# A DeltaNet and MLP kernel: the second MLP product as seven products of blocks, with its sums on GpSimd, other DMA queues, and the inverse's rows behind marked adds

## The chip, the cores and the metric

The kernel runs on one core of a Trainium2 chip. The metric is device time in microseconds, the median of three runs. All data is fp32.

## The reference

What is computed, cut to the lines that matter (B, H, S, D = 4, 8, 768, 48; the model width is H * D = 384 and the hidden width 1536):

```python
k_n = k / (np.linalg.norm(k, axis=-1, keepdims=True) + 1e-06)
state = 0                                   # (B, H, D, D)
for t in range(S):
    y[:, :, t] = einsum('bhd,bhde->bhe', q[:, :, t], state)
    v_old = einsum('bhde,bhd->bhe', state, k_n[:, :, t])
    state = state + beta[t] * einsum('bhd,bhe->bhde', k_n[:, :, t], v[:, :, t] - v_old)
x = y as (B, S, H * D)
xn = (x - mean(x)) / sqrt(var(x) + 1e-06) * g_ln
out = x + maximum(xn @ w_ch1, 0) @ w_ch2
```

## The kernel before, in words

The sequence is cut into 12 chunks of 64 tokens. Two chunks make a slab. For each chunk the recurrence over its 64 tokens is turned into matrix products with the inverse of a triangular matrix, for all 32 pairs of batch and head. The chunk's tokens of all four batches (256 rows) then go through layer norm and the MLP.

The stages, by name:

- **Loads.** `load_turned` fetches keys and queries of a chunk in small blocks (tile `tb`, line 168), the keys on GpSimd's queue and the queries on SP's. `load_kv` fetches keys and values (lines 184, 175) on SP. `turned` (L348) transposes `tb` into `kqt` on VectorE.
- **Gram matrices.** `gram` (L368) multiplies keys by keys into `p_g`; ScalarE copies them to `gsb` (L376, L383). `product` (L393, L395) does the same for keys and queries and masks the result into `pt`.
- **Inverse.** `blocks` and `inverse` (L477 to L560) invert the 32x32 triangles of a slab on VectorE, one row at a time: a product into `tmp` (L555), a subtraction from `xb` (L560), each with two SBUF inputs, 31 times, two rows to a step. `scatter` (L483, L468, L472) turns the result into `xt`. `join` (p_e L580, p_z L626) then combines two 32x32 triangles into the 64x64 one on TensorE.
- **Recurrence.** `recur`: p_k and p_y from the state (L652), `v_raw` minus p_k on VectorE (L657), p_u (L663), p_s (L675) and its add to the state `s_all` on VectorE (L678), p_y (L683), layer norm (L694 to L701), the transposes p_n (L709) into `xnt`.
- **MLP.** `ffn`: for each of 12 blocks of the hidden width, p_h = W1 block by `xnt`, 3 products of 128x256 (L724), and ScalarE's ReLU into `h_f` (L730). Then h W2: for each half of 128 rows, 12 products of 128x384 that add up in one PSUM tile p_o (L746); VectorE adds x (L735) and SP's queue stores `o` (L737). Chunk 0 does both halves together. The PSUM tiles p_h and p_o share a pool with two buffers.

The norms of the keys (L411 to L420) and the scaling of v by them (L428, on GpSimd) are prepared a chunk or more ahead.

What sets the order: `Plan` is a list of due times, in units of which one chunk has T = 45. Every stage is a generator with a number of steps spread over a stretch of the plan; the steps are traced in the order of their due times, and the scheduler of the framework orders each engine's instructions by this priority and by when it believes them ready. An engine runs its queue strictly in the order so fixed. `tc.issue_after(ins)` puts what is traced in a block behind `ins` on `ins`'s engine; `behind_each(tc, last, gen)` does so for every step of a generator, with the instructions that `last` holds at that moment. Before the change only `join` is so treated, behind the MLP's latest product.

The lines of the plan that the change and the prediction speak of:

```python
times = (t - 70, t - 58, t - 18, t - 13) if m > 2 else (t - 56, t - 46, t - 18, t - 13)
plan.spread(in_turn(*(prep_g(c) for c in chunks)), SLAB * 2, times[0], times[1])
plan.spread(blocks(m), N_BLOCKS, times[1], times[2])
joining = join(chunks)
plan.spread(joining if m == 1 else behind_each(tc, mlp, joining), 3, times[3], t - 2)
```

Here t is the start of the slab's first chunk in the plan and m is the slab.

## Time and profile before

| what | value |
|---|---|
| median of 3 runs | 614.44 us (612.59 to 615.7) |
| span of the profiled execution | 613.5 us |
| passes of p_h (L724), 128x256 | 864, busy 206.9 us |
| passes of p_o (L746), 128x384 | 576, busy 201.2 us |
| VectorE's rows (L555 and L560) | 42.3 and 51.1 us busy |
| GpSimd: v by its norm (L428), 128x768 | 10 of 1.476 us |
| GpSimd: key loads (L168) | 64, busy 42.6 us |
| DMA | 34.51 MB, 56 GB/s over the span |

How to read it: PE is TensorE's products and PEld its weight loads, which run beside them; DVE is VectorE, ACT ScalarE, POOL GpSimd, SP the queue of SyncE. A product of fp32 shows as two records. The mean length of a matmul's record is a latency, and records overlap, so what one costs is read from a stretch in which nothing else runs. A group's line gives busy time and mean length, then the engine's idle time just before it and what ended that idle time.

### The profile page before, as it was taken

The numbers are of one execution on the slowest core, as the hardware profiler recorded it, in microseconds if no ns is written. First come the engines' busy times: TensorE is split into PE (matmuls) and PEld (weight loads), VectorE is DVE, ScalarE is ACT, GpSimd is POOL, SyncE is SP. The second block draws the span as 40 slices with busy tenths as digits, with TensorE's granted clock in tenths as the row PEclk, the third lists the DMA queues.
The fourth block names the chain that finished last, engine by engine and source line by source line (L and its number), as shares of the span: only waits on it lengthen the run. The fifth ranks groups of instructions, "written<-read, shape, count | busy, mean of one in ns | idle before, by whom it ended". The sixth has DMA issues, their size and how long they took to land.

```text
span 613.5 us, 20905 instructions
## 1 busy us (share of the span) xinstructions
PE 540.2 (88%) x9512; PEld 403.8 (66%) x9512; DVE 322.7 (53%) x681; ACT 170.4 (28%) x351; POOL 80.7 (13%) x128
## 2 busy tenths in 40 slices
PE   2046886988999959999999999999999999999997
PEld 2035765556767846866767867768768678677673
DVE  5846868992246992239964059952179720201000
ACT  1223242402333214241224242242322142122120
POOL 5000116321041202300303200011000010000000
PEclk9999878998999979999999999999999999999999
DMA  4817889326044601411600500200200000000101
GB/s 54 199 50 164 172 179 243 56 52 95 3 97 62 103 8 24 74 34 28 104 16 17 101 16 15 53 16 15 53 14 15 1 22 9 14 15 1 27 1 26
DMA packets 126919, 34.51 MB, mean 56 GB/s; under 512 B 121184, under 2 KB 124272, under 8 KB 126832
## 3 DMA queue, kind: packets, MB, share of 16 engines
q1 hardware_dynamic: 110256, 19.14, 18.7%
q0 software_dynamic: 3504, 10.25, 6.0%
q10 hardware_dynamic: 13072, 3.80, 2.7%
q8 instruction: 74, 1.21, 0.8%
q14 instruction: 13, 0.11, 0.1%
HBM read 28.44 MB, written 4.72 MB: 54 GB/s over the span
## 4 chain that ended last, share of the span: by engine, by line
PE 55%; DVE 28%; issue 6%; DMA 3%; ACT 3%; SPq 3%; POOL 1%; ACTq 0%; DVEq 0%; POOLq 0%
PE p_o L746 19%; PE p_h L724 19%; DVE tmp L555 8%; DVE xb L560 8%; SPq L168 2%; PE p_g L368 2%; PE p_y L683 2%; PE p_e L580 2%; DVE kqt L348 2%; PE p_z L626 2%; PE p_g L393 1%; PE p_u L663 1%; DVE own L483 1%; PE p_n L709 1%; PE p_s L675 1%
## 5 line engine op out<-in xcount | busy, mean ns | idle before, releaser
L724 PE MATMUL p_h<-xnt,w_sb 128*128 128x256 f32 x864 | 206.9, 393 | 5.9 <-DVE o L735 5.2
L746 PE MATMUL p_o<-w_sb,h_f 128*128 128x384 f32 x576 | 201.2, 498 | 0.0
L724 PEld LDWEIGHTS p_h<-xnt,w_sb 128*128 128x128 f32 x864 | 164.4, 195 | 34.0 <-DVE o L735 4.0
L746 PEld LDWEIGHTS p_o<-w_sb,h_f 128*128 128x128 f32 x576 | 107.4, 193 | 65.6 <-issue 3.0
L730 ACT ACTIVATE h_f<-p_h 128x256 f32<-128x256 f32 x144 | 55.3, 384 | 192.4 <-PE p_h L724 192.3
L168 POOL DMA_DIRECT2D tb<-in_k_dram x64 | 42.6, 673 | 110.8 <-DVE tmp L555 57.3
L560 DVE TENSOR_TENSOR xb<-xb,tmp 128x31 f32<-128x31 f32 (+20 forms) x154 | 51.1, 332 | 5.1
L735 DVE TENSOR_TENSOR o<-p_o,x_ln 128x384 f32<-128x384 f32 x24 | 13.2, 549 | 74.0 <-PE p_o L746 74.0
L555 DVE TENSOR_TENSOR tmp<-xb,gb 128x31 f32<-128x31 f32 (+15 forms) x124 | 42.3, 341 | 3.8
L694 DVE BATCH_NORM_STATS2 st<-x_ln 128x6 f32<-128x384 f32 x24 | 12.3, 547 | 49.4 <-ACT x_ln L688 49.4
L678 DVE TENSOR_TENSOR s_all<-s_all,p_s 128x768 f32<-128x768 f32 x11 | 10.4, 942 | 47.2 <-PE p_s L675 47.1
L348 DVE STREAM_TRANSPOSE kqt<-tb 128x1024 f32<-128x1024 f32 x24 | 29.3, 1232 | 4.1 <-DMA tb<-in_k_dram 3.8
L368 PE MATMUL p_g<-kqt 48*64 48x64 f32 (+2 forms) x1024 | 16.8, 239 | 12.3 <-DVE kqt L348 8.2
L368 PEld LDWEIGHTS p_g<-kqt 48*32 48x32 f32 (+1 forms) x1024 | 14.8, 133 | 17.8 <-DVE kqt L348 8.3
L610 PE MATMUL p_e<-x_n,gsb 32*32 32x16 f32 x512 | 6.0, 187 | 21.6 <-DVE x_n L605 17.3
L420 POOL TENSOR_SCALAR knrm<-knrm 128x16 f32<-128x16 f32 x12 | 3.1, 257 | 163.1 <-ACT knrm L419 163.1
L417 DVE TENSOR_REDUCE ksum<-ksq 128x8 f32<-128x384 f32 x22 | 12.1, 550 | 21.2 <-ACT ksq L411 10.9
L580 PE MATMUL p_e<-x_n,gsb 32*32 32x32 f32 x768 | 16.1, 200 | 7.7 <-DVE mv L695 5.8
L580 PEld LDWEIGHTS p_e<-x_n,gsb 32*32 32x32 f32 x768 | 14.7, 113 | 11.0 <-DVE x_n L574 6.0
L393 PEld LDWEIGHTS p_g<-kqt 48*64 48x64 f32 x768 | 14.0, 142 | 11.9 <-DVE s_all L678 6.4
L657 DVE TENSOR_TENSOR v_raw<-v_raw,p_k 128x768 f32<-128x768 f32 x11 | 10.5, 952 | 20.8 <-PE p_k L652 20.8
L393 PE MATMUL p_g<-kqt 48*64 48x64 f32 x768 | 16.5, 231 | 5.1 <-DVE s_all L678 3.8
(99 smaller groups left out, 509.9 us busy)
## 6 DMA issues: line engine op xcount, KB each, us to landing
words<-in_moe_w_ch_dram POOLq DMA_DIRECT2D x9, 768.0 KB, 5.9
out_dram<-o SPq DMA_DIRECT2D x48, 96.0 KB, 2.2
k<-in_k_dram SPq DMA_DIRECT2D x44, 96.0 KB, 2.8
v_raw<-in_v_dram SPq DMA_DIRECT2D x22, 192.0 KB, 4.0
tb<-in_q_dram SPq DMA_DIRECT2D x44, 64.0 KB, 3.0
words<-in_moe_w_ch_dram ACTq DMA_DIRECT2D x3, 768.0 KB, 6.4
tb<-in_k_dram POOLq DMA_DIRECT2D x32, 64.0 KB, 3.4
tb<-in_q_dram SPq DMA_DIRECT2D x44, 32.0 KB, 2.6
```

The costliest lines, as they stand in the source:

```text
L168: engs[m % len(engs)].dma_start(out=dst[p0 : p0 + 32, :, u, 0:w], in_=src[:, hp::2, toks, 32 * m : 32 * m + w].rearrange("b j t d -> t (b ...
L348: nc.vector.transpose(made[c][0][:, :, n].rearrange("p i (u t) -> p i u t", t=32), tblocks[(2 * c + n) % NTB])
L368: nc.tensor.matmul(out_, kqt[rows, i, 0, r0 : r0 + (BK if fine else C)], kqt[rows, i, 0, r0:C])
L393: nc.tensor.matmul(p_g[half(e ^ hp), hp, j], kqt[rows, i, 0], kqt[rows, i, 1])
L555: nc.vector.tensor_tensor(out=t, in0=xb[:, :, 0:n, j : j + 1].to_broadcast([128, nb, n, w]), in1=gb[:, :, j : j + 1, j + 1 : L].to_broadca ...
L560: nc.vector.tensor_tensor(out=rest, in0=rest, in1=t, op=ALU.subtract)
L580: nc.tensor.matmul(p_e[r1, h], gsb[r0, h, BK:C], xn[r0, h])
L694: nc.vector.bn_stats(out=st[:, g], in_=y[:, g])
L724: nc.tensor.matmul(p_h, w1_sb[:, t, f * 128 : (f + 1) * 128], xnt[:, t], start=(t == 0), stop=(t == KC - 1),)
L730: nc.scalar.activation(h_f, p_h, ACTF.Relu)
L735: nc.vector.tensor_tensor(out=o, in0=p_o, in1=x[:, g], op=ALU.add)
L746: nc.tensor.matmul(p_o, hs[f][:, g * 128 : (g + 1) * 128], w2_sb[:, f], start=(f == 0), stop=(f == FT - 1),)
```

## The change

Five edits:

1. **h W2 as seven products.** For chunks 1 to 11, h (256 rows by 1536) and W2 (1536 by 384) are cut into 2 x 2 blocks, and the product is formed by Winograd's form of Strassen's scheme: seven products of blocks in place of eight. A block product is 6 products of 128x192 for one half of the rows, one half of the hidden width and one half of the output columns. The sums of W2's blocks (t1 to t4) are made once by `sum_blocks`; the sums of h's blocks (s1 to s4) are made per chunk; both on GpSimd. VectorE adds the products to x in eight adds of 128x192. The PSUM tile p_a holds three products on top of one another; p_c and p_b are two halves of one tile, in one bank. h is kept in two tiles of six blocks each.
2. **Key loads** of `load_turned` go to SP's queue.
3. **Stores** of the result go to GpSimd's queue, except the last chunk's.
4. **The inverse's rows queue behind what TensorE waits for.** `soon()` marks a VectorE instruction (the subtraction of p_k, the add to `s_all`, the normalised rows, the adds of the MLP); each step of `blocks` is queued behind the one marked last.
5. **The plan:** T from 45 to 43, gram matrices and rows due up to 4 units later.

```diff
     def load_turned(c):
-        load_blocks(k, c, 0, (nc.gpsimd,))
+        load_blocks(k, c, 0, (nc.sync,))
         load_blocks(q, c, 1, (nc.sync,))
...
             nc.vector.tensor_tensor(out=v_j, in0=v_j, in1=p_k, op=ALU.subtract)
+            soon()
...
             nc.vector.tensor_tensor(out=s_all, in0=s_all, in1=p_s, op=ALU.add)
+            soon()
...
                 op0=ALU.subtract, op1=ALU.mult,
             )
+        soon()
...
-    N_FFN = FT + 2 * FT // 2
+    HF, HM = FT // 2, DM // 2
+    N_FFN = FT + 7 * 2
+    sums = []
+
+    def sum_blocks():
+
+        late = ctx.enter_context(tc.tile_pool(name="late", bufs=1))
+        b11, b12, b21, b22 = (w2_sb[:, i : i + HF, j : j + HM] for i in (0, HF) for j in (0, HM))
+        t2, t3, t4 = (late.tile([128, HF, HM], FP32, name=f"t{i}") for i in (2, 3, 4))
+        for t, x0, x1 in ((t3, b22, b12), (b12, b12, b11), (t2, b22, b12), (t4, b21, t2)):
+            nc.gpsimd.tensor_tensor(out=t, in0=x0, in1=x1, op=ALU.subtract)
+        sums.extend((late, b12, t2, t3, t4))
...
+    urgent = {}
+
+    def soon():
+        urgent["DVE"] = nc.cur_bb.bb.instructions[-1]
...
-            h_f = work.tile([128, TOK], FP32, name="h_f", bufs=FT)
-            nc.scalar.activation(h_f, p_h, ACTF.Relu)
-            hs.append(h_f)
+            nc.scalar.activation(h[f // HF][:, f % HF], p_h, ACTF.Relu)
...
+                (nc.gpsimd if c < NCH - 1 else nc.sync).dma_start(
+                    out=out[2 * e + g, c * C : (c + 1) * C, :], in_=os[g][e * C : (e + 1) * C]
                 )
...
+        def add(out_, in0, in1):
+            nc.vector.tensor_tensor(out=out_, in0=in0, in1=in1, op=ALU.add)
+            soon()
...
+        a11, a21, a12, a22 = (h[i][:, :, g * 128 : (g + 1) * 128] for i in range(2) for g in range(2))
+        late, t1, t2, t3, t4 = sums
+
+        s1, s2, s3, s4 = a21, a11, late.tile([128, HF, 128], FP32, name="s3"), a12
...
+        p_a, p_cb = ps_ffn([128, HM], "p_a"), ps_ffn([128, DM], "p_o")
+        p_c, p_b = p_cb[:, 0:HM], p_cb[:, HM:]
...
+        def mul(p, a, b, first):
+            for f in range(HF):
+                nc.tensor.matmul(
+                    p, a[:, f], b[:, f], start=(first and f == 0), stop=(f == HF - 1), skip_group_check=True,
+                )
+                mlp["PE"] = nc.cur_bb.bb.instructions[-1]
+                if f == HF // 2 - 1:
+                    yield
+
+        sum_of(s3, a11, a21, ALU.subtract)
+        sum_of(s1, a21, a22, ALU.add)
+        yield from mul(p_a, a11, w11, True)
+        add(o11, p_a, x11)
+        sum_of(s2, s1, a11, ALU.subtract)
+        yield
+        yield from mul(p_c, a12, w21, True)
+        add(o11, p_c, o11)
+        sum_of(s4, a12, s2, ALU.subtract)
+        yield
+        yield from mul(p_b, s1, t1, False)
+        add(o22, p_b, x22)
+        yield
+        yield from mul(p_a, s2, t2, False)
+        add(o12, p_a, x12)
+        yield
+        yield from mul(p_b, s4, w22, False)
+        add(o12, p_b, o12)
+        store(0)
+        yield
+        yield from mul(p_a, s3, t3, False)
+        add(o22, p_a, o22)
+        add(o21, p_a, x21)
+        yield
+        yield from mul(p_c, a22, t4, True)
+        add(o21, p_c, o21)
+        store(1)
+        yield
...
-    T = 45
+    T = 43
...
+    plan.once(42, sum_blocks)
...
-            times = (t - 70, t - 58, t - 18, t - 13) if m > 2 else (t - 56, t - 46, t - 18, t - 13)
+            times = (t - 70, t - 54, t - 14, t - 13) if m > 2 else (t - 56, t - 42, t - 14, t - 13)
...
-            plan.spread(blocks(m), N_BLOCKS, times[1], times[2])
+            plan.spread(behind_each(tc, urgent, blocks(m)), N_BLOCKS, times[1], times[2])
```

More of the change, by code (lines that the diff above doesn't have):

```diff
@@ L711, in recur @@
         yield
-    N_FFN = FT + 2 * FT // 2
+    HF, HM = FT // 2, DM // 2
[8 more added lines that the diff above has]
+        sums.extend((late, b12, t2, t3, t4))
     mlp = {}
+    urgent = {}
+    def soon():
+        urgent["DVE"] = nc.cur_bb.bb.instructions[-1]
     def ffn(c):
         xnt, x = xnts.pop(c), xs.pop(c)
-        hs = []
+        h = [work.tile([128, HF, TOK], FP32, name="h") for _ in range(2)]
         for f in range(FT):
@@ L728, in ffn, with store @@
             mlp["PE"] = nc.cur_bb.bb.instructions[-1]
-            h_f = work.tile([128, TOK], FP32, name="h_f", bufs=FT)
-            nc.scalar.activation(h_f, p_h, ACTF.Relu)
-            hs.append(h_f)
+            nc.scalar.activation(h[f // HF][:, f % HF], p_h, ACTF.Relu)
             yield
-        def store(g, p_o):
-            o = work.tile([128, DM], FP32, name="o", bufs=2)
-            nc.vector.tensor_tensor(out=o, in0=p_o, in1=x[:, g], op=ALU.add)
+        os = [work.tile([128, DM], FP32, name="o", bufs=2) for g in range(2)]
+        def store(g):
             for e in range(2):
-                nc.sync.dma_start(
-                    out=out[2 * e + g, c * C : (c + 1) * C, :], in_=o[e * C : (e + 1) * C]
-                )
-        for gs in ((0, 1),) if c == 0 else ((0,), (1,)):
-            p_os = [ps_ffn([128, DM], "p_o") for g in gs]
+                (nc.gpsimd if c < NCH - 1 else nc.sync).dma_start(
+                    out=out[2 * e + g, c * C : (c + 1) * C, :], in_=os[g][e * C : (e + 1) * C]
+                )
+        def add(out_, in0, in1):
+            nc.vector.tensor_tensor(out=out_, in0=in0, in1=in1, op=ALU.add)
+            soon()
+        if c == 0:
+            p_os = [ps_ffn([128, DM], "p_o") for g in range(2)]
             for f in range(FT):
-                for g, p_o in zip(gs, p_os):
+                for g in range(2):
                     nc.tensor.matmul(
-                        p_o, hs[f][:, g * 128 : (g + 1) * 128], w2_sb[:, f],
+                        p_os[g], h[f // HF][:, f % HF, g * 128 : (g + 1) * 128], w2_sb[:, f],
                         start=(f == 0), stop=(f == FT - 1),
@@ L752, in ffn, with sum_of @@
                     yield
-            for g, p_o in zip(gs, p_os):
-                store(g, p_o)
+            for g in range(2):
+                add(os[g], p_os[g], x[:, g])
+                store(g)
             yield
+            return
+        a11, a21, a12, a22 = (h[i][:, :, g * 128 : (g + 1) * 128] for i in range(2) for g in range(2))
+        late, t1, t2, t3, t4 = sums
+        s1, s2, s3, s4 = a21, a11, late.tile([128, HF, 128], FP32, name="s3"), a12
+        def sum_of(out_, in0, in1, op):
+            nc.gpsimd.tensor_tensor(out=out_, in0=in0, in1=in1, op=op)
+        p_a, p_cb = ps_ffn([128, HM], "p_a"), ps_ffn([128, DM], "p_o")
+        p_c, p_b = p_cb[:, 0:HM], p_cb[:, HM:]
+        x11, x12, x21, x22 = (x[:, g, n : n + HM] for g in range(2) for n in (0, HM))
+        o11, o12, o21, o22 = (os[g][:, n : n + HM] for g in range(2) for n in (0, HM))
+        w11, w21, w22 = w2_sb[:, 0:HF, 0:HM], w2_sb[:, HF:, 0:HM], w2_sb[:, HF:, HM:]
+        def mul(p, a, b, first):
[34 more added lines that the diff above has]
+        yield
     NW = len(pieces)
```

## The prediction

> **What bounds the kernel now.** I read the page's busy shares first, then the costliest groups, then the chain, then busy time by stretch, then TensorE's waits.
>
> From the page of the kernel before (parts 1 and 5):
>
> ```profile
> PE 540.2 (88%) x9512; PEld 403.8 (66%) x9512; DVE 322.7 (53%) x681; ACT 170.4 (28%) x351; POOL 80.7 (13%) x128
> ...
> L746 PE MATMUL p_o<-w_sb,h_f 128*128 128x384 f32 x576 | 201.2, 498 | 0.0
> ...
> L746 PEld LDWEIGHTS p_o<-w_sb,h_f 128*128 128x128 f32 x576 | 107.4, 193 | 65.6 <-issue 3.0
> ```
>
> TensorE leads. L746 is h W2: 576 records for 12 chunks x 12 blocks x 2 halves = 288 products, so each fp32 product is two passes. The 498 ns is a latency; passes overlap, so it is no price. The price comes from the chain in order of time, whose last two pieces run with nothing in between (start, length, what):
>
> ```profile
> 577.98 15.54 PE p_h L724 x72
> 593.52 15.49 PE p_o L746 x48
> ```
>
> 15.54/72 = 215.8 ns for a pass of 256 columns, 15.49/48 = 322.7 ns for 384. The difference is 0.835 ns a column and the rest 2.0 ns: TensorE is paced by columns and the weight loads are wholly hidden.
>
> Busy time by stretch, from one start of p_k to that two chunks later, then the last recurrences (bounds; length; PE, PEld, DVE, ACT, POOL busy; clock; DMA share; GB/s):
>
> ```profile
> 245.10:332.30 87.20, 84.88 (x1408) 63.00 (x1411) 50.26 (x110) 26.40 (x55) 14.77 (x21) 1.00 0.27 47
> 332.30:419.50 87.20, 84.73 (x1408) 63.04 (x1408) 50.30 (x110) 26.39 (x55) 9.61 (x13) 1.00 0.20 38
> ...
> 506.40:544.10 37.70, 37.70 (x451) 28.10 (x450) 5.29 (x11) 7.37 (x17) 0.00 (x0) 1.00 0.05 12
> ```
>
> A steady pair of chunks costs 87.2 us and TensorE idles 2.3 to 2.5 us of it. So the steady state is TensorE's, and the 28% of VectorE on the chain are mostly stretches where the two run side by side. TensorE's waits from 160 to 560 us (total, times, longest):
>
> ```profile
> PE p_e L580 <- DVE mv L695: 5.8, 1, 5.8
> PE p_g L393 <- DVE s_all L678: 3.8, 3, 1.4
> PE p_h L724 <- DVE o L735: 2.8, 3, 0.9
> ```
>
> All three are VectorE being late. The first is the second pair, where p_e waits for the transposed inverse. The other two are adds that TensorE waits for while the rows of the inverse stand in front of them.
>
> **What the Trainium skill says.** "TensorE: Matmul & The Clock Gate", LDWEIGHTS, prices a load at its columns over 1.2 GHz, 107 ns for 128. The trace has six transposes with one 128-column load each, about 109 ns apart (p_n: 0.82 us from first start to last end, 0.27 of it the latency of one), which agrees, though a transpose may load faster than a product. "SBUF — State Buffer", two separate sides, says that GpSimd and VectorE share a port pair as an exclusive lock, held for a whole instruction, against VectorE operations with two SBUF inputs. The trace agrees (timeline of the kernel before: start, length, engine, instruction):
>
> ```profile
> 128.49 0.29 DVE L560 TENSOR_TENSOR xb<-xb,tmp 128x126 f32<-128x126 f32 x1
> ...
> 128.97 1.48 POOL L428 TENSOR_TENSOR v_raw<-v_raw,knrm 128x768 f32<-128x768 f32 x1
> 129.13 1.46 DVE L560 TENSOR_TENSOR xb<-xb,tmp 128x120 f32<-128x120 f32 x1
> ```
>
> A row that takes 0.29 us takes 1.46 us and ends 0.14 us after GpSimd's product does. "PSUM — Partial Sum Buffer", bank collisions, wants PSUM guarded by bank, not by address. No wait of the kernel before shows two products in one bank.
>
> **The change part by part.**
>
> *h W2 as seven products (chunks 1 to 11).* Removed: 24 products of 384 columns, 48 passes x 322.7 = 15.49 us. Added: 7 x 6 = 42 products of 192 columns, 84 passes. By the line above a pass is 0.835 x 192 + 2.0 = 162.3 ns, so 13.63 us, if a load of 128 columns still hides. Lower bound of the load: 107 ns. Upper: loads of 64 columns in four tiles of the array (p_u, 64 in 1.08 us, so 16 per tile at 67.5 ns with their products) give at most 135 ns for 128. The worst reading is the whole latency, 190 ns. I take hidden: -1.86 us a chunk, -20.4 us for eleven. Chunk 0 is unchanged.
>
> *Adds on VectorE.* Two of 549 ns become eight of 192 columns. From 549 (384 columns) and 421 (own+p_z, 256) the slope is 1.0 ns, so 357 ns each: 2.86 - 1.10 = +1.76 us a chunk. VectorE would be at 53.8 of some 82 us a pair, so as a sum it is hidden.
>
> *Sums on GpSimd.* Four of 128x768, priced by L428 (1.475 us): 5.9 us a chunk on an engine with 10 to 15 us of work in 87. TensorE hides them: the first two products (3.9 us) need no sum; s3 needs only the first half of h; s1 is done about 2 us after h, s2 at about 3.5 us (needed at 5.9), s4 at about 5.5 us (needed at 7.8). The price falls on VectorE through the lock: up to 5.9 us of delay a chunk where rows run. The block sums of W2 (4 of 128x1152, some 2.2 us each by 1.92 ns an element) fall between the last reading of W2 by chunk 0 (131 us) and chunk 1's third product (after 167 us): hidden, with perhaps 1 to 3 us of lock before the p_e at 138.86.
>
> *A new wait in one bank.* p_c and p_b share a bank. If the wait is by bank, the third product waits for the add that reads the second: 0.2 us to drain, 0.36 us add, 0.05 us to restart, so 0.6 us a chunk, 6.6 us in all, if VectorE is free and nothing stands between. The plan puts other TensorE work into some of these gaps: I take half, +3.3. The other adds have one or two products (1.95 or 3.9 us) of room.
>
> *Rows behind the urgent adds.* The waits for s_all (3.8) and o (2.8) are taken away: -6.6. What queues behind each marked add is the next two rows (up to 1.8 us) and so the inverse, for which p_e waits. In the pair before 419 us, the second gram starts at 357.67 and ends at 358.75, x_n is done at 398.03 and p_e starts at 403.79: 39.3 us of chain and 5.8 us to spare. The plan has 48.3 units between that gram (t-59.5) and the join (t-11.2), 46.1 us as run. After: 44.8 units (gram at t-56), and with 84.8 - 3.7 = 81.1 us of TensorE for 86 units, 42.3 us. The chain gets +1.8 (adds), +2.4 (normalisation, which ran at 399 to 402, behind it) and 0 to 5.9 of lock: 43.5 to 49.4 us. It is late by 1.2 to 7.1 us a pair, unless TensorE has other products to run first, which near the end of a chunk it mostly has. I take 1.5 us for each of the three steady pairs and 1.5 more on the 5.8 of the second: +6.0.
>
> *Loads and stores.* Keys on SP: 8 more issues of about 0.6 us a chunk (SP's q loads: 13 in 7.95), some 13 us in 41; they run a chunk or more ahead: 0. Stores on GpSimd, 0.65 us an issue as its key loads have: SP no longer holds loads behind a store that waits for o (SP's q loads at 190.79 came right behind one at 188.85), and keys leave GpSimd in exchange: 0 for the sum, perhaps -1 in the second pair. T from 45 to 43 only moves the order.
>
> Sum: 614.4 - 20.4 + 3.3 - 6.6 + 6.0 = 596.7, so 597 us.
>
> **The rivals.**
>
> *All of it lands:* the adds come at once, the inverse stays ahead, the bank's wait lies beside other work: 614.4 - 20.4 - 6.6 = 587.4, about 588 us. For it: TensorE has 97% of the steady pairs. Against it: the chain's slack of 5.8 us is spent.
>
> *The inverse becomes the bound (slower):* the lock costs all of 5.9 us and TensorE has nothing else. Then 7.1 us for each of three pairs, as much more in the second, and the whole 6.6 of the bank: 614.4 - 20.4 - 6.6 + 28.4 + 6.6 = 622 us. For it: between 364 and 398 us VectorE is busy 31.87 of 34 us, and the lock is seen at 129. Against it: a row's order is chosen beside the products, and p_u comes well after p_e.
>
> *The weight loads show (slower):* a pass costs 190 ns, so 84 x 0.190 = 15.96 us, +0.47 a chunk, +5.2 in all; with +3.3, -6.6, +6.0 this is 622 us. Against it: the 109 and 67.5 ns above.
>
> **How the numbers follow.** Forecast 0.50, all lands 0.27, inverse bound 0.16, loads show 0.05, something in the order that I don't see 0.02. Within 0.5% is 611.4 to 617.5: between forecast and inverse bound, 0.09. Slower 0.14, faster 0.77. The range goes from 584 (all lands, and 3 us of the ramp through freer queues) to 614 (half-way to the inverse as bound); what is left out is the slower cases and a little below.
>
> **What would show it.** The last 84 passes in 13.6 us, in place of 48 in 15.5, show the price of a pass; 16 us would show the loads. Records of p_a and p_cb that wait for an add after the second product show the bank. The lines for s_all and o among TensorE's waits should be gone. A wait of p_e for x_n in every pair, and rows of 1.5 us beside GpSimd's sums, would show the inverse as the bound. The prediction fails if TensorE falls under 93% in the steady pairs, or if a sum comes late to its product.

## The result and the profile after

The change makes the kernel slower: 638.35 us median (636.51 to 641.14, 4 runs) against 613.52 us (611.08 to 615.7, 4 runs) for the kernel before on the same chip. The ratio is 1.041, with a 95% interval of 1.0351 to 1.0468. The forecast was 597 us, with a range of 584 to 614. Where single microseconds are compared below, they come from the profiled executions: a span of 613.5 us before and 639.4 us after. Each ratio compares a kernel's runs with those of the kernel before that were taken beside it (medians 615.4 to 616.5 us in the experiments), without the runs that are over 1.5% above the same kernel's quickest, so that where times spread, the median of all runs can lie above what the ratio says.

The page of the kernel after, parts 1 and 5. A group's line gives engine, operation, output <- inputs, shape and count, then busy time and mean ns, then the engine's idle time just before and what ended it:

```profile
PE 540.9 (85%) x9908; PEld 471.9 (74%) x9908; DVE 371.2 (58%) x747; ACT 169.9 (27%) x351; POOL 153.2 (24%) x156
...
L788 POOL TENSOR_TENSOR h<-h 128x768 f32<-128x768 f32 x33 | 60.1, 1821 | 129.0 <-ACT h L747 89.6
...
L560 DVE TENSOR_TENSOR xb<-xb,tmp 128x31 f32<-128x31 f32 (+20 forms) x154 | 61.8, 401 | 4.6
L555 DVE TENSOR_TENSOR tmp<-xb,gb 128x31 f32<-128x31 f32 (+15 forms) x124 | 54.0, 436 | 3.4
...
L788 POOL TENSOR_TENSOR s<-h 128x768 f32<-128x768 f32 x11 | 20.1, 1831 | 79.4 <-ACT h L747 79.4
```

Three things are to be seen. TensorE is as busy as before (540.9 us against 540.2), although 11 chunks have 1.86 us less of products each. GpSimd's sums take 1.82 us each, not 1.475. And the rows of the inverse, whose number and shapes have not changed, take 115.8 us (61.8 + 54.0) where they took 93.4 (51.1 + 42.3).

That the products themselves got cheaper is plain at the end of the chain in order of time (start, length, what):

```profile
631.12 1.95 PE p_a L798 x12
633.07 1.96 PE p_o L798 x12
```

12 passes of 128x192 in 1.95 us are 162.5 ns a pass; 162.3 was forecast. Busy time by stretch, with the columns of the forecast (bounds; length; PE, PEld, DVE, ACT, POOL busy; clock; DMA share; GB/s), for one steady pair of chunks and for the chunk after the last rows:

```profile
351.30:444.90 93.60, 85.29 (x1483) 75.87 (x1484) 58.53 (x122) 26.35 (x56) 23.16 (x21) 0.95 0.20 36
...
536.00:571.90 35.90, 35.90 (x487) 32.74 (x487) 6.89 (x17) 7.35 (x17) 9.37 (x8) 1.00 0.06 13
```

The second line is what the change was made for: 35.9 us in place of 37.7, TensorE never idle. There are no rows there. The first line is a pair with rows: 93.6 us in place of 87.2. TensorE idles 8.3 us of it (93.60 - 85.29) and its clock is 0.95. Its products should have kept TensorE busy for 84.7 - 3.7 = 81.0 us; it was busy for 85.3. So I put 4.3 us down to the lower clock and 5.8 us to more idling than the 2.5 of before: 87.2 - 3.7 + 4.3 + 5.8 = 93.6.

TensorE's waits from 160 to 572 us (total, times, longest), against 5.8, 3.8 and 2.8 us before:

```profile
PE p_g L393 <- DVE s_all L679: 12.2, 3, 5.4
PE p_e L580 <- DVE x_n L574: 11.6, 4, 4.1
PE p_o L798 <- DVE o L759: 6.2, 5, 3.0
```

All are VectorE being late, as before, but 30.0 us where those three lines had 12.4. The third is not the wait for `o` of before: that one was p_h's, and it fell from 2.8 to 0.9 us. This one is new. All five times it is the third block product (p_b) that waits until the add has read the second (p_c), the other half of the same tile; more on it below. Why VectorE is late can be read where the first of the pair's two long waits begins. VectorE's timeline of the kernel after (start, length, instruction):

```profile
408.96 0.38 DVE L560 TENSOR_TENSOR xb<-xb,tmp 128x207 f32<-128x207 f32 x1
409.37 1.84 DVE L555 TENSOR_TENSOR tmp<-xb,gb 128x192 f32<-128x192 f32 x1
411.25 1.84 DVE L560 TENSOR_TENSOR xb<-xb,tmp 128x192 f32<-128x192 f32 x1
413.02 0.94 DVE L679 TENSOR_TENSOR s_all<-s_all,p_s 128x768 f32<-128x768 f32 x1
```

GpSimd's timeline in the same stretch:

```profile
409.19 3.69 POOL L788 TENSOR_TENSOR h<-h 128x768 f32<-128x768 f32 x2 [8.57 <-ACT h L747]
```

TensorE's:

```profile
414.01 1.16 PE L393 MATMUL p_g<-kqt 48*64 48x64 f32 x64 [3.43 <-DVE s_all L679]
415.10 1.90 PE L798 MATMUL p_o<-w_sb,h 128*128 128x192 f32 x6
...
428.19 1.92 PE L580 MATMUL p_e<-x_n,gsb 32*32 32x32 f32 x64 [4.06 <-DVE x_n L574]
```

A row has two instructions of 0.38 us. Two sums start at 409.19, and for as long as they run the row's two instructions take 1.84 us each, 3.68 us in all beside GpSimd's 3.69. The add to `s_all` stands behind that row and comes 2.9 us later than it could, and TensorE has nothing else in front: it idles 3.43 us. The 64 products of p_g that come next still take 1.16 us, as at full clock; then six passes take 1.90 us where they take 1.14. After 4.06 us of idling, 64 products of p_e take 1.92 us where they take 1.20. That is the lower clock of the pair: the granted clock is 0.50 from 416 to 418 us and from 428 to 432 us. The Trainium skill has both halves of this: "SBUF — State Buffer", two separate sides (the lock, which the loser waits for to the end), and "TensorE: Matmul & The Clock Gate", What's actually happening, which puts the array at half its clock after an idle window of about 3.4 us. The two waits here are 3.43 and 4.06 us, and the trace agrees. But 3.4 us is no limit below which a wait is safe: in the kernel e1 below, 2.72 us of idling are followed by half clock as well (64 products of p_e in 1.92 us), while 2.45 us in e17 are not.

The same happens once more, early. VectorE in the ramp, at the first step of the second slab's inverse:

```profile
119.28 2.27 DVE L541 TENSOR_SCALAR nrm<-nrm 128x32 f32<-128x32 f32 x1 [0.32 <-ACT nrm L540]
...
122.19 2.49 DVE L545 TENSOR_TENSOR db<-db,beta_f 128x32 f32<-128x32 f32 x1
124.72 3.23 DVE L546 TENSOR_TENSOR xb<-xb,db 128x512 f32<-128x512 f32 x1
127.88 2.65 DVE L549 COPY xb<-db 128x32 f32<-128x32 f32 x1
```

These four stand beside the four sums of W2's blocks, which GpSimd runs from 118.70 to 130.47 us at 2.64 to 2.99 us each. Without neighbours the second, third and fourth take 0.19, 0.69 and 0.19 us (a kernel below shows it).

Where the 25.9 us lie, by stretch between starts of p_k, with two kernels from the experiments beside it (in after and e11 a part of chunk 4's p_k runs ahead; the start of the rest is taken):

| stretch (us) | before | after | after, no sums (e11) | half of the chunks (e9) |
|---|---|---|---|---|
| start to chunk 2 | 167.3 | 174.8 | 164.0 | 165.6 |
| chunk 2 to 4 | 77.7 | 82.6 | 77.3 | 73.4 |
| 4 to 6 | 87.2 | 93.8 | 86.1 | 84.8 |
| 6 to 8 | 87.2 | 93.6 | 87.8 | 84.9 |
| 8 to 10 | 86.9 | 91.2 | 85.6 | 84.2 |
| 10 to 11 (no rows) | 37.7 | 35.9 | 35.9 | 35.9 |
| 11 to the end | 69.4 | 67.5 | 65.7 | 67.5 |
| span | 613.5 | 639.4 | 602.4 | 596.3 |

The sums cost something even where no rows are left: in the last stretch the two normalised blocks of rows (L703) stand beside three sums and take 3.19 us, where e11 has 0.87.

### The profile page after: what moved, and what is told of

Same layout as the page of the kernel before. It is cut to its first block, busy times and chain, and to the rows that moved or that the text cites. A ratio compares the mean times of both kernels' runs of the same rounds, so it can differ in the third digit from the quotient of the medians.

```text
span 639.4 us, 21859 instructions
## 1 busy us (share of the span) xinstructions
PE 540.9 (85%) x9908; PEld 471.9 (74%) x9908; DVE 371.2 (58%) x747; ACT 169.9 (27%) x351; POOL 153.2 (24%) x156
## 4 chain that ended last, share of the span: by engine, by line
PE 50%; DVE 34%; issue 7%; ACT 3%; DMA 3%; POOL 1%; ACTq 0%; SPq 0%; DVEq 0%; POOLq 0%
PE p_h L742 20%; DVE tmp L555 9%; DVE xb L560 9%; PE p_o L798 8%; PE p_a L798 7%; PE p_e L580 2%; PE p_z L626 2%; PE p_g L368 2%; DVE o L759 2%; DMA tb<-in_k_dram 1%; PE p_y L685 1%; PE p_u L664 1%; DMA words<-in_moe_w_ch_dram 1%; DVE own L483 1%; DVE gb L477 1%
## 5 line engine op out<-in xcount | busy, mean ns | idle before, releaser
L747 ACT ACTIVATE h<-p_h 128x256 f32<-128x256 f32 x144 | 55.2, 383 | 181.5 <-PE p_h L742 181.4
L788 POOL TENSOR_TENSOR h<-h 128x768 f32<-128x768 f32 x33 | 60.1, 1821 | 129.0 <-ACT h L747 89.6
L798 PE MATMUL p_o<-w_sb,h 128*128 128x192 f32 x396 | 79.6, 349 | 6.6 <-DVE o L759 6.2
L798 PEld LDWEIGHTS p_o<-w_sb,h 128*128 128x128 f32 x396 | 69.4, 202 | 8.8 <-DVE o L759 6.1
L560 DVE TENSOR_TENSOR xb<-xb,tmp 128x31 f32<-128x31 f32 (+20 forms) x154 | 61.8, 401 | 4.6
L555 DVE TENSOR_TENSOR tmp<-xb,gb 128x31 f32<-128x31 f32 (+15 forms) x124 | 54.0, 436 | 3.4
L754 POOL DMA_DIRECT2D out_dram<-o x44 | 24.0, 549 | 85.5 <-DVE o L759 50.4
L759 DVE TENSOR_TENSOR o<-p_a,x_ln 128x192 f32<-128x192 f32 x33 | 11.6, 352 | 51.5 <-PE p_a L798 51.4
L788 POOL TENSOR_TENSOR s<-h 128x768 f32<-128x768 f32 x11 | 20.1, 1831 | 79.4 <-ACT h L747 79.4
L393 PE MATMUL p_g<-kqt 48*64 48x64 f32 x768 | 19.2, 253 | 19.5 <-DVE s_all L679 12.2
L798 PE MATMUL p_a<-t,h 128*128 128x192 f32 x132 | 28.7, 363 | 1.4 <-DVE o L759 1.0
L580 PEld LDWEIGHTS p_e<-x_n,gsb 32*32 32x32 f32 x768 | 16.1, 121 | 16.1 <-DVE x_n L574 12.1
L759 DVE TENSOR_TENSOR o<-p_o,o 128x192 f32<-128x192 f32 x33 | 11.4, 345 | 25.1 <-PE p_o L798 24.9
```

The source lines that it names most:

```text
L393: nc.tensor.matmul(p_g[half(e ^ hp), hp, j], kqt[rows, i, 0], kqt[rows, i, 1])
L555: nc.vector.tensor_tensor(out=t, in0=xb[:, :, 0:n, j : j + 1].to_broadcast([128, nb, n, w]), in1=gb[:, :, j : j + 1, j + 1 : L].to_broadca ...
L560: nc.vector.tensor_tensor(out=rest, in0=rest, in1=t, op=ALU.subtract)
L580: nc.tensor.matmul(p_e[r1, h], gsb[r0, h, BK:C], xn[r0, h])
L747: nc.scalar.activation(h[f // HF][:, f % HF], p_h, ACTF.Relu)
L754: (nc.gpsimd if c < NCH - 1 else nc.sync).dma_start(out=out[2 * e + g, c * C : (c + 1) * C, :], in_=os[g][e * C : (e + 1) * C])
```

## The experiments

The theory that I took from the two traces (the lock): GpSimd's sums stop VectorE whenever they meet it, and VectorE is what TensorE waits for. The rivals: the order of VectorE's work (eight adds, rows queued behind marks), the queues, the plan's due times, and, later, the seven products themselves.

### The sums taken away, and their waits kept

In e1 the four sums of h per chunk are left out; the products read the blocks of h as they are. The instructions on VectorE, ScalarE and SP and their order are the same as in the kernel after.

```diff
-        s1, s2, s3, s4 = a21, a11, late.tile([128, HF, 128], FP32, name="s3"), a12
+        s1, s2, s3, s4 = a21, a11, a11, a12
...
-            nc.gpsimd.tensor_tensor(out=out_, in0=in0, in1=in1, op=op)
+            pass
```

> The changed kernel without the four sums of h's blocks on GpSimd: s1 to s4 are left out, so TensorE multiplies the blocks of h as they are and the output is not the reference's. The queues of VectorE, ScalarE and SP are the same, instruction by instruction. Lock theory (GpSimd's sums hold the port that VectorE's rows need, the inverse comes late, TensorE idles and its clock falls): 598 to 610 us, VectorE's rows (L555 and L560) fall from 115.8 us to about 105 (the block sums of W2 still stretch slab 1's), steady pairs fall from 93.6 to 82 to 86 us. Order theory (the rows queued behind marked adds, and due 4 units later, are what makes the inverse late): 630 to 640 us.

Measured: 612.49 us, ratio 0.9931 (0.9904 to 0.9957). The page of e1:

```profile
L560 DVE TENSOR_TENSOR xb<-xb,tmp 128x31 f32<-128x31 f32 (+20 forms) x154 | 49.8, 324 | 4.6
L555 DVE TENSOR_TENSOR tmp<-xb,gb 128x31 f32<-128x31 f32 (+15 forms) x124 | 42.1, 340 | 3.4
```

The rows are back at 91.9 us. So nothing in the order, the queues or the plan made them longer. The time is 2.5 us above what the lock theory expected, and the pairs, at 87.3, 86.9 and 85.2 us, are above its 82 to 86: the sums are most of the loss, but something is left.

In e2 each sum is replaced by two memsets of the same tile (the sums are left out of the computation here too). The waits of the products for GpSimd stay, and GpSimd is busy 65.0 us with them (88 memsets of 0.74 us), but a memset reads nothing.

```diff
-            nc.gpsimd.tensor_tensor(out=out_, in0=in0, in1=in1, op=op)
+            nc.gpsimd.memset(out_, 0.0)
+            nc.gpsimd.memset(out_, 0.0)
```

> Each of the four sums of h's blocks is replaced by two memsets of the same tile (128x768) on GpSimd: the blocks hold zeros and the output is not the reference's, but TensorE still waits for GpSimd at the same four places, and GpSimd is busy for nearly as long. A memset reads nothing from SBUF. Lock theory: as without the sums, 598 to 612 us, no rows of 1.8 us. Wait theory (TensorE waits for GpSimd's sums as such): 625 us or more.

Measured: 617.02 us, ratio 0.9994 (0.9957 to 1.0032), 0.6% above e1, with the rows at 323 and 340 ns. This lies between the two expectations, 5 us above the one and 8 below the other. Being busy and being waited for is worth some 0.6% (two memsets take 1.48 us where a sum takes 1.82); the 4% from there to the kernel after come only with sums that read.

### The sums added to the kernel before

The counter-proof is e12: the kernel before, with four idle sums of 128x768 on GpSimd per chunk that nobody reads, in chunks 1 to 11. Its own products, adds, queues and plan stay.

```diff
+            for _ in range(4):
+                nc.gpsimd.tensor_tensor(
+                    out=scratch[0], in0=hs[FT - 1][:, None, :].to_broadcast([128, 3, TOK]),
+                    in1=w1_sb[:, 0, 0 : 3 * TOK].rearrange("p (a b) -> p a b", a=3), op=ALU.subtract,
+                )
```

> The kernel before with four sums of 128x768 added on GpSimd for each of chunks 1 to 11, of h's last block and a weight tile, whose results nobody reads; the products, adds, plan and queues of before. Lock theory: the rows beside the sums wait as in the kernel after, and the chain's spare 5.8 us are not enough for what the sums take (20 us over the run): 619 to 640 us. Rival (sums cost only what waits for them, as the products of after do): 613 to 616 us, since nobody waits for these.

Measured: 632.45 us, ratio 1.0268 (1.0221 to 1.0315). The sums alone make the kernel before slower, by about two thirds of what the whole change does. In the profiled run most of it lies in two stretches: chunk 2 to 4 (5.9 us) and the last pair with rows (7.9 us). The key loads, which stand behind the sums in GpSimd's queue here, are not the cause: VectorE waits 4.1 us for them over the run, 3.8 us in the kernel before. Its VectorE in the last pair, before TensorE's longest wait:

```profile
491.41 1.71 DVE L468 TENSOR_SCALAR xt<-own,is_u 128x512 f32<-128x512 f32 x1
493.05 2.02 DVE L472 COPY xt<-own 128x512 f32<-128x512 f32 x1
494.99 2.02 DVE L468 TENSOR_SCALAR xt<-own,is_u 128x512 f32<-128x512 f32 x1
496.93 2.02 DVE L472 COPY xt<-own 128x512 f32<-128x512 f32 x1
...
499.49 0.91 DVE L678 TENSOR_TENSOR s_all<-s_all,p_s 128x768 f32<-128x768 f32 x1
```

Its GpSimd:

```profile
491.04 7.62 POOL L739 TENSOR_TENSOR scratch<-h_f,w_sb 128x768 f32<-128x768 f32 x4 [33.99 <-ACT h_f L731]
```

Its TensorE:

```profile
500.46 1.99 PE L393 MATMUL p_g<-kqt 48*64 48x64 f32 x64 [7.40 <-DVE s_all L678]
```

Four instructions of 0.41 to 0.57 us in the kernel before (same lines, at 395 us) take 7.8 us beside four sums, one for one, and TensorE waits 7.4 us. L472 is a plain copy of one tile, so it isn't only instructions with two tiles as inputs that the sums stop.

### The sums of W2's blocks

In e10 one thing is moved: the four block sums are queued on GpSimd behind the start of the first inverse (after the memset of `es`) and no longer run at 118.7 us.

```diff
-    plan.once(42, sum_blocks)
+    def late_sums():
+        with behind(tc, joined):
+            sum_blocks()
+
+    plan.once(56, late_sums)
```

> The kernel after with one edit: the four sums of W2's blocks are queued on GpSimd behind the start of the first inverse, so that they do not run beside the second slab's first rows. Lock theory: the +7.5 us that the trace shows up to chunk 2's p_k become 0 to +2, and the steady pairs stay, so 629 to 634 us (ratio about 1.028). Rival (the ramp is late through the key loads on SP or through the first chunks' own adds): unchanged, 636 to 642 us.

Measured: 630.14 us, ratio 1.0243 (1.0201 to 1.0284). The ramp ends at 163.4 in place of 174.8 us. VectorE in e10, the instructions that were shown above:

```profile
117.03 0.19 DVE L545 TENSOR_TENSOR db<-db,beta_f 128x32 f32<-128x32 f32 x1
117.26 0.69 DVE L546 TENSOR_TENSOR xb<-xb,db 128x512 f32<-128x512 f32 x1
117.87 0.19 DVE L549 COPY xb<-db 128x32 f32<-128x32 f32 x1
```

So four sums at a bad moment, once in the run, cost 1.7%. The steady pairs stay at 93.9, 93.5 and 91.2 us, as they should.

In e11 neither the sums of h nor those of W2's blocks are left (the products read the blocks as they are).

```diff
-        t2, t3, t4 = (late.tile([128, HF, HM], FP32, name=f"t{i}") for i in (2, 3, 4))
-        for t, x0, x1 in ((t3, b22, b12), (b12, b12, b11), (t2, b22, b12), (t4, b21, t2)):
-            nc.gpsimd.tensor_tensor(out=t, in0=x0, in1=x1, op=ALU.subtract)
-        sums.extend((late, b12, t2, t3, t4))
+        sums.extend((late, b12, b22, b22, b21))
```

> The kernel after with neither the sums of h nor those of W2's blocks (its products read blocks of h and W2 as they are, so the output is not the reference's). Lock theory: against the kernel without the sums of h (ratio 0.993) the ramp's 5 to 7 us come as well: 603 to 607 us, ratio 0.982 to 0.988; what is then still missing to 594 (= 614.4 - 20.4) is the inverse's chain with its later start and p_e's waits of 2 to 3 us a pair. Rival (the block sums cost nothing): 0.990 to 0.996 again.

Measured: 607.09 us, ratio 0.9852 (0.9813 to 0.9891), as expected. From 1.041 to 0.985: all sums together cost 5.6% of the run, some 34 us. The rest, from 0.985 to the forecast's 0.97, is not the sums'.

### What the lock is not: queues, marks, the engine for the sums

e6 takes key loads and stores back to the queues of before.

```diff
-        load_blocks(k, c, 0, (nc.sync,))
+        load_blocks(k, c, 0, (nc.gpsimd,))
...
-                (nc.gpsimd if c < NCH - 1 else nc.sync).dma_start(
+                nc.sync.dma_start(
```

> The changed kernel with key loads on GpSimd's queue and stores on SP's, as before the change; the sums are in. Lock theory: 630 to 648 us, the queues hardly matter. Queue theory (stores in front of sums in GpSimd's queue delay them, or keys on SP come late): under 625 us.

Measured: 646.3 us, ratio 1.0496 (1.043 to 1.0563), not faster than the kernel after. The queues are no cause of its loss.

e3 has the kernel after with rows no longer queued behind the marks:

```diff
-            plan.spread(behind_each(tc, urgent, blocks(m)), N_BLOCKS, times[1], times[2])
+            plan.spread(blocks(m), N_BLOCKS, times[1], times[2])
```

> The changed kernel with the inverse's rows not queued behind the marked adds; all else stays. Lock theory: 625 to 645 us, since GpSimd's sums still stretch the rows. Order theory: 605 to 618 us.

Measured: 642.57 us, ratio 1.041 (1.0352 to 1.0468), the same as with marks, though other waits make it up: TensorE waits 27.7 us for `s_all` here, the longest 8.5. e4 does the converse and adds the marks and the queueing to the kernel before:

> The kernel before with one edit of the change: its rows queued behind the marked VectorE instructions (subtraction of p_k, add to s_all, normalised rows, add of x). Lock theory: 606 to 616 us, a gain of up to the 6.6 us of waits for s_all and o, or none. Order theory: 625 us or more.

Measured: 612.68 us, ratio 0.9979 (0.9951 to 1.0008). The marks neither cost nor bring anything that shows there.

e7 moves the sums of h to VectorE, as marked work:

```diff
-            nc.gpsimd.tensor_tensor(out=out_, in0=in0, in1=in1, op=op)
+            nc.vector.tensor_tensor(out=out_, in0=in0, in1=in1, op=op)
+            soon()
```

> The four sums of h's blocks on VectorE, marked like the adds, in place of GpSimd; the block sums of W2 stay on GpSimd. A sum of 128x768 is some 0.95 us there (as s_all), so 3.8 us a chunk of VectorE's own time in place of up to 7.3 us of lock. Lock theory: 612 to 628 us, no rows of 1.8 us. Rival (it is the amount of work before the rows that counts, wherever it runs): 632 us or more.

Measured: 620.62 us, ratio 1.0008 (0.9968 to 1.0048), though its runs spread from 610.5 to 627.3 us and the ratio of the medians is 1.007. The page of e7 has 44 sums in 42.5 us (951 and 1011 ns), and the rows at 322 and 339 ns. To do the sums on VectorE itself, 4 us a chunk, costs the run 3 to 4% less than to do them on GpSimd "beside" it: there a sum takes 1.82 us and VectorE can lose as much.

### What is still missing without any sum

e11 saves 1.8 to 3.7 us in the two last stretches, but its pairs with rows take 85.6 to 87.8 us, hardly less than the 86.9 to 87.2 of before, though each has 3.7 us less of products. The prediction's working offered the length of the inverse's chain, or the new bank and adds. In e5 the kernel e1 gets the plan of before (T 45, old due times):

```diff
-    T = 43
+    T = 45
...
-            times = (t - 70, t - 54, t - 14, t - 13) if m > 2 else (t - 56, t - 42, t - 14, t - 13)
+            times = (t - 70, t - 58, t - 18, t - 13) if m > 2 else (t - 56, t - 46, t - 18, t - 13)
```

> As e1 (the sums of h's blocks left out, output not the reference's), with T and the due times of the plan before (T 45, gram and rows due 4 units earlier). In e1 TensorE still waits 2.2 to 2.7 us a pair for x_n. Plan theory (the later due times took the inverse's slack): 594 to 603 us and no wait of p_e for x_n in the steady pairs. Rival (the eight adds a chunk on VectorE took it): 605 to 613 us, the wait stays.

Measured: 620.6 us, ratio 1.0081 (1.0053 to 1.011): neither; it is slower than e1. TensorE now waits 20.0 us for `o`, four times, the longest 6.1, and each time it is again p_b that waits for the add on p_c. The old plan as a whole is no help to the seven products.

e13 and e14 shorten the chain alone. Every second row of the inverses of chunks 4 to 11 is cut to one row of its matrix, which leaves a part of the inverse out; the instructions stay. e13 does that in the kernel after, e14 in e11.

```diff
-            n, w = j + 1, L - 1 - j
+            n, w = 1 if L > FB and j % 2 else j + 1, L - 1 - j
```

> The kernel after, with every second row of the inverses of chunks 4 to 11 cut to one row of its matrix (the instructions stay, the output is not the reference's): about half of VectorE's 23 us of rows for a pair, all sums left in. If the sums and the lock cost time only because the inverse's chain is longer than the pair, TensorE's pace comes back though the sums are still there: pairs near 83 to 86 us where after has 93 to 94, and 598 to 614 us in all (the ramp's 7 us, which belong to the first slab, stay). If the sums cost by themselves (TensorE waits for s1 to s4, or the adds that it waits for stand in the lock), the pairs stay above 89 us and the whole above 618.

> The same cut of rows in the kernel without any sums (ratio 0.985, whose steady pairs take 86 to 87 us where 81 to 83.5 were worked out). If what it still lacks is the inverse's chain (second gram to x_n in 42.7 us, and p_e 2.7 us late), the pairs fall to 81.5 to 84 us and the whole to 585 to 595 us (ratio 0.955 to 0.97). If it is the seven products themselves (the bank that p_c and p_b share, weight loads, restarts after eight adds), the rows don't matter: 602 to 608 us.

Measured: e13 1.0 (0.9957 to 1.0043), e14 0.9697 (0.9627 to 0.9768). Both spread widely (e13 609.5 to 625.3 us; e14 593.0 once and 600.8 to 601.7 three times), and by medians the ratios are 1.009 and 0.976. With half of the rows' work the sums still cost some 3%, where they cost 5.6% with all: their price goes with what they meet. In the three pairs of the profiled runs it shows best: e13 (619.6 us, near its median) takes 265.5 us for them and e14 260.3, so the sums cost 5 us there, where with all rows they cost 19 (278.5 after, 259.5 in e11). That e14 is at the upper end of what was expected is not a success of the expectation, though: its pairs take 88.0, 86.7 and 85.7 us, no less than e11's. It gains from chunk 2 to 4 (71.1 us in place of 77.3), where the inverse is indeed what TensorE waits for, and in the profiled run 6 us before any edited instruction. p_e waits for x_n as it did:

```profile
PE p_e L580 <- DVE x_n L574: 7.4, 3, 2.7
```

(e14, 229 to 490 us; the line of e11 for its three pairs is the same to the digit, though e14 has half of the rows' work.) So in the steady pairs it is not the length of the chain. The trace of e14 shows where the wait comes from: the last row's two instructions are queued behind a marked add and the normalisation, VectorE idles 1.86 us ahead of them, and then 5 us of transposition and copies to xt lie between them and x_n. That is a place in the order, so three kernels move it. e17 is e11 with rows due until t-18 as before:

```diff
-            times = (t - 70, t - 54, t - 14, t - 13) if m > 2 else (t - 56, t - 42, t - 14, t - 13)
+            times = (t - 70, t - 54, t - 18, t - 13) if m > 2 else (t - 56, t - 42, t - 18, t - 13)
```

> The kernel without any sums (ratio 0.985), with one edit: the rows of the inverse are due until t-18, as in the kernel before, and not until t-14; they start as late as in the kernel after, and T stays 43. If the rest that halving the rows did not remove is the place of the inverse's last rows in VectorE's order (behind a marked add and the normalisation, with VectorE idle ahead of them), p_e's waits for x_n (five, 2.7 us the longest) go or shrink below 1 us, the pairs come to 84 to 85 us, and the ratio to 0.970 to 0.980. If it is not the place, the waits stay, and the ratio is 0.983 to 0.99; if the rows now stand in front of adds that TensorE needs, waits for s_all or o come in their place and it is above 0.99.

e18 is e11 with T 44 and rows due from t-58 (t-46) to t-18:

> The kernel without any sums with the plan of the kernel that has the products only beside no rows: T 44, rows due from t-58 to t-18 (t-46 to t-18 for the third slab). If the plan is what made that one reach 0.967 with seven chunks of products in place of eleven, this comes to 0.965 to 0.975, with no wait of p_e for x_n above 1 us. If the plan is of no use to eleven chunks (as it was not with T 45, where TensorE waited 20 us for o), the ratio is 0.985 to 1.0, with such waits again.

e15 is e11 without the marks (the edit of e3):

> The kernel without any sums, rows no longer queued behind the marked adds. If the marks are a good part of the chain's 42.7 us, p_e's waits for x_n (10 us in all) go and others come for s_all and o: within 3 us of the kernel without sums, 601 to 609 us, with the waits moved. If marks only delay, it gets faster by 3 to 8 us: 596 to 602. If they are what keeps TensorE going, it gets slower: above 611.

Measured: 0.9884 (0.9854 to 0.9913), 0.9883 (0.9826 to 0.9939) and 0.9873 (0.9824 to 0.9923), beside 0.9852 for e11: four orders, one time. For e17 the waits of its third reading came with the ratio of the second. TensorE's waits in e17, 239 to 503 us:

```profile
PE p_o L795 <- DVE o L756: 12.1, 3, 4.8
```

In e15, 240 to 537 us:

```profile
PE p_g L393 <- DVE s_all L679: 8.5, 3, 3.7
```

In the pairs the waits of p_e are gone in both (and in e18, with 10.6 us for `o`), and another has come in the place of each: once a pair, TensorE waits 2.2 to 4.8 us for whichever add stands in or behind the inverse's end. VectorE in e17 while TensorE waits (from 394.2 to 399.02):

```profile
391.49 2.08 DVE L483 STREAM_TRANSPOSE own<-xb 128x1024 f32<-128x1024 f32 x1
393.61 1.25 DVE L468 TENSOR_SCALAR xt<-own,is_u 128x512 f32<-128x512 f32 x1
...
395.84 1.21 DVE L395 TENSOR_TENSOR pt<-p_g,pmask 128x1024 f32<-128x1024 f32 x1
396.97 1.29 DVE L574 STREAM_TRANSPOSE x_n<-xt 128x512 f32<-128x512 f32 x2
...
398.63 0.33 DVE L756 TENSOR_TENSOR o<-p_o,o 128x192 f32<-128x192 f32 x1
```

Some 7 us of VectorE's work with no add of the MLP among it, and then the 0.33 us that TensorE stands for. What TensorE stands with can be read from its own order in the same stretch:

```profile
389.74 1.24 PE L795 MATMUL p_o<-w_sb,h 128*128 128x192 f32 x6
...
391.99 1.24 PE L795 MATMUL p_o<-w_sb,h 128*128 128x192 f32 x6
393.06 1.14 PE L795 MATMUL p_a<-w_sb,h 128*128 128x192 f32 x6
399.02 1.33 PE L795 MATMUL p_o<-w_sb,h 128*128 128x192 f32 x3 [4.81 <-DVE o L756]
```

The first two lines are the second product (p_c), the third is half of the fourth (p_a, run ahead), and the last is the third product, p_b. It writes other columns than p_c and uses no result of that add; what the two have in common is the tile, in one bank. So I read it as the wait in one bank that the prediction named. All three waits of this line in e17, the four of e5 and the three of e18's pairs are of this kind. The two halves of the plain product, with one add behind 24 passes (7.7 us) each, have no such wait. What a version with p_c and p_b in two banks would take was not run.

### Seven products only where no rows stand

If both the lock and this wait need rows on VectorE, the products belong into the chunks beside which there are none: 1, 3, 5, 7, 9, 10 and 11. Chunks 2, 4, 6 and 8 get their plain 24 products back. e8 does this, with the block sums placed as in e10, T 44 and rows due as before; its plain chunks read a W2 whose block b12 is overwritten by t1, so they leave the right b12 out. e9 has a tile of its own for t1, and two buffers of `pt` in place of three for the room.

```diff
+    PLAIN = (2, 4, 6, 8)
...
+        if c in PLAIN:
+            for g in range(2):
+                p_o = ps_ffn([128, DM], "p_o")
+                for f in range(FT):
+                    nc.tensor.matmul(
+                        p_o, h[f // HF][:, f % HF, g * 128 : (g + 1) * 128], w2_sb[:, f],
+                        start=(f == 0), stop=(f == FT - 1),
+                    )
...
-    T = 43
+    T = 44
```

> A version built on the theory: seven products only for the chunks whose sums don't fall beside the inverse's rows (1, 3, 5, 7, 9, 10, 11), the plain product for 2, 4, 6 and 8, block sums of W2 queued behind the inverse of the first slab, due times of before with T 44. Lock theory: 7 x 1.86 = 13 us less than before, 596 to 606 us. If something else in the change costs (adds, queues, rows behind): 610 us or more.

> The kernel after with the seven products only where no rows of the inverse stand on VectorE (chunks 1, 3, 5, 7, 9, 10, 11; chunks 2, 4, 6, 8 take the plain 24 products), the sums of W2's blocks queued behind the first inverse's start, t1 in a tile of its own with pt at two buffers in exchange, T 44 and the due times of before. Lock theory: chunk by chunk 1.86 us for seven chunks are gained (13 us) and the lock falls on fewer rows: 596 to 604 us where before is 614. Rival (the adds, the queues and the new due times are what costs): at least 610 us, since all of these are still there.

Measured: e8 597.52 us, ratio 0.971 (0.9665 to 0.9754); e9 596.21 us, ratio 0.9674 (0.9629 to 0.972). This version is faster than both kernels. e9 by stretch:

```profile
239.00:323.80 84.80, 83.64 (x1445) 67.94 (x1444) 52.87 (x118) 27.95 (x59) 17.64 (x19) 1.00 0.36 57
323.80:408.65 84.85, 83.62 (x1442) 67.90 (x1441) 51.96 (x116) 26.35 (x55) 15.92 (x17) 1.00 0.22 40
408.65:492.90 84.25, 83.39 (x1443) 67.80 (x1442) 48.34 (x112) 24.68 (x51) 13.24 (x14) 1.00 0.10 21
```

TensorE idles about 1.2 us of a pair or less, and the clock is 1.00. The sums are still on GpSimd (21 of 1812 ns and 7 of 1836), and the rows are at 324 and 344 ns: they hardly meet. With seven chunks of products in place of eleven it gets more than e11 with no sums at all.

In e16, e9 without the marks:

> The kernel with the seven products only beside no rows (ratio 0.967), rows no longer queued behind the marked adds. The same three readings: marks neutral 594 to 599 us; marks only delay 588 to 594; marks needed 600 to 608. This also says which of the two is the version to keep.

Measured: 604.71 us, ratio 0.9791 (0.9741 to 0.984). So here the marks are worth 1.2% of the run: without them TensorE waits 7.3 us for `s_all` between 160 and 560 us, with them 2.2. Alone they were worth nothing (e4).

## Why the prediction was wrong

**The price of the products: right.** 162.3 ns a pass were worked out, 162.5 measured; a chunk with no rows beside it gains 1.8 us (37.7 to 35.9), and at 162.5 ns the loads stay hidden. The adds are right as well: 352 and 345 ns where 357 was taken. The rival of the weight loads is out.

**The sums on GpSimd: the step that failed.** The prediction wrote "the price falls on VectorE through the lock: up to 5.9 us of delay a chunk where rows run", and then carried of it only what the inverse's chain would be late: +6.0 us in all, 1.5 a steady pair, beside a -6.6 for waits that would go. A steady pair came out 6.4 to 6.6 us longer in place of shorter. Four things were wrong in that.

1. Its duration. The nearest row, L428 with 1.475 us, multiplies by a value repeated along the row; a sum of two full blocks takes 1.82 us, 7.3 us a chunk.
2. Whom it hits. The prediction named operations with two inputs in SBUF. The same section of the Trainium skill, "SBUF — State Buffer", two separate sides, also names VectorE's two-port modes. In the traces instructions with one input stand still too: copies (L472), multiplications by a column (L468), the addition of a constant (L541); in which mode they ran no trace shows. And it hits what stands behind: `s_all` was 2.9 us late through one row. The term "-6.6" for the waits of `s_all` and `o` was taken as sure. p_h's wait for `o` did fall, from 2.8 to 0.9 us, but the one for `s_all` grew from 3.8 to 12.2. Without sums (e11) both are at 0.9: the term was near right, and the lock undid it. A mark helps only against the rows queued behind it, not against one that is already waiting for the lock.
3. Its size on TensorE. The chain was worked out as 43.5 to 49.4 us. In the pair before 445 us the second gram ends at 379.08 and x_n is done at 428.14: 49.1 us. So the chain came out at the upper end of the prediction's own sum. The prediction took 1.5 us a pair for it, since TensorE "mostly has" other products near the end of a chunk. It had not: in that pair it waited 4.1 us for x_n and 3.4 us for `s_all`, and idled 8.3 us in all.
4. What idling costs besides. After each of the pair's two waits TensorE ran at half clock for a while: 4.3 us more of PE busy in that pair. No term of the sum had it.

Together the steady pairs became 6.6, 6.4 and 4.3 us longer, where the terms of the prediction make them some 3 to 4 us shorter.

**The sums of W2's blocks: wrong place.** They were put between 131 us and some time after 167 us, "hidden, with perhaps 1 to 3 us of lock". They ran from 118.7 us, as soon as VectorE had made the last block of W2 (the second waited only for chunk 0's product), and stood on the first step of an inverse. They took 2.64 to 2.99 us each where 2.2 was worked out. The ramp was 7.5 us longer, and to move them alone gave 1.7% of the run.

**The wait in one bank: the right place, too small under load.** The prediction gave it 0.6 us a chunk "if VectorE is free and nothing stands between", 6.6 us in all, and took half. In the kernel after it is 6.2 us, the longest 3.0; in e17 it is 12.1 us and in e5 20.0. The condition was what failed: in the pairs with rows VectorE is not free.

**The inverse's chain: right as a danger, wrong as a cause by itself.** With no sums the chain still ends late for p_e (2.7, 2.7 and 2.0 us in the three pairs), which the taken 1.5 us is near to. But halving the rows did not change this. It is the inverse's end that collides with what TensorE needs from VectorE, and every order tried for it has such a wait: p_e for x_n in e11, p_b for the add on p_c in e17 and e18, p_g for `s_all` in e15. The working counted VectorE's time (+1.76 us a chunk, "as a sum it is hidden"), but not that some 7 us of VectorE's work can stand in front of one add of 0.33 us.

**Loads and stores: right at zero,** or a little on the good side: with the old queues the kernel after takes 1.0496 (1.043 to 1.0563), with the new ones 1.041. T was moved only together with the due times of the rows (e5, e18), so what it does alone is not shown.

Of the rivals, "the inverse becomes the bound" has the right mechanism and, with 622 us, two thirds of the result's distance too little (+7.6 us in place of +24.8): it left out the ramp (7.5 us), the clock, and the sums' true length. It was given 0.16. Its own marks in the section "What would show it" came: rows of over 1.5 us beside the sums and waits of p_e for x_n in every pair. TensorE was at 91% in two of the three steady pairs (85.29 of 93.60 us in the one shown), under the 93% at which the prediction said it would fail. A sum came late to its product only once, by 0.4 us.

## What to carry to other kernels

In these runs a GpSimd instruction that reads SBUF stood in the place of VectorE's work on SBUF, for as long as GpSimd took: price each such instruction at its full length on whatever VectorE has to do in that moment, and on all that is queued behind it. Adds that read PSUM were spared: at 420.27 us one took 0.34 us beside a sum, and the row behind it 1.59. If VectorE feeds TensorE, put the work where VectorE's queue is short (here 0.967 in place of 1.041 with the same sums in seven of the eleven chunks), or do it on VectorE itself. A saving of products that is paid with more adds in between needs a look at the longest unbroken piece of other work on the adding engine, not at its total, and at which product shares a tile with one that an add still has to read; and a wait of several microseconds has to be priced with the slow clock after it.

## What the runs showed of the hardware that I had not expected

- VectorE's smallest instructions with one input are stopped as well: the addition of a constant on 128x32 took 2.27 us, a copy of 128x32 2.65 us (0.19 alone), copies of 128x512 2.02 us (0.41 alone), each ending as a GpSimd sum does. In a dense queue this goes one for one: four instructions in 7.8 us beside four sums in 7.6.
- A GpSimd memset does not stop the rows, which have two inputs: with 88 memsets of 0.74 us they kept their 323 and 340 ns. It does stop an instruction with one input: the multiplication L468 that begins at 393.61 us in e17 takes 1.25 us beside a memset of 0.95 (393.63), the same one without it 0.47.
- A sum of 128x768 on GpSimd costs 1.82 us, on VectorE 0.95 us, and the product by a repeated value (L428) 1.48 us on GpSimd.
- Half clock came after waits of 3.43 and 4.06 us (1.16 us later in the first case, at once in the second), and also after 2.72 us in e1 and 2.34 in e16 (64 products of p_g in 1.99 us in place of 1.16).
